# Adding transfers or vector sums for three outer sums, and one or two levels in the last down product of an expert

## The chip, the cores and the metric

The kernel runs on one core of a Trainium2 chip. The metric is the device time of one execution in microseconds, median of several runs. TensorE (PE) multiplies, VectorE (DVE), ScalarE (ACT) and GpSimd (POOL) do the elementwise work, SyncE (SP) issues plain transfers, and POOL issues the transfers that add to what lies at their destination. All data is float32.

## The reference, cut to what matters

```
kv  = einsum('bhsd,bhse->bhde', k, v)          # 8 x 8 heads, 576 rows, 64 columns
o   = einsum('bhsd,bhde->bhse', q, kv)
x   = (o / sqrt(mean(o*o, -1) + 1e-6) * g_norm)   # reshaped to 4608 x 512
p   = domain_probs / (domain_probs.sum(-1) + 1e-9)
out = 0
for e in range(4):
    h    = maximum(x @ w1[e], 0)               # 512 -> 1024: the "up" product
    out += p[:, e] * (h @ w2[e])               # 1024 -> 512: the "down" product
```

Almost all the time goes into the up and the down products of the four experts.

## The kernel before

The 4608 rows of x are cut into 9 chunks of 512. One step s = 9 e + c is expert e on chunk c, so there are 36 steps, 0 to 35. A step has an up product (`up`, line 851 on) and a down product, and the down product of step s runs beside the up product of step s + 1.

Both products use Strassen's scheme: 7 products of blocks in place of 8, with sums of blocks before and after. The up product uses it at two levels from step 1 on: 7 outer products m, in the order 1, 2, 6, 5, 3, 7, 4, each made of 7 inner products mm of two instructions (line 891). For one outer product, ScalarE copies four results out of the up banks of PSUM (`u1`, `u2`; L910) and one seed into another bank, and VectorE adds two others (`total`, L918) into one buffer, `made[m]`. The outer sums then join whole buffers of 128 x 1024:

- after m = 2: h1 = made1 + made2, then a Relu in place (L874)
- after m = 6: made1 and made6 are added, and later v, from that sum and made5
- after m = 4: h2 = made1 + made4, then a Relu
- others make h21, h4, h7, h5, h6, h3; these always are sums of VectorE, or of VectorE or GpSimd, whichever the planner finds free (`combine`, L360).

The down product has two forms. `down` (line 1100 on) is one level: 14 products of four instructions with 256 columns (L1118), whose results are scaled by p and merged straight out of PSUM (ACT L1065, DVE L1072) into the output blocks. `down_deep` (line 1140 on) is two levels: 98 instructions for the same, of 128 columns (L1193), with sums of h before them (L360), copies and sums out of PSUM (L1221, L1229) and sums of outer products after them (L1259). Both send output blocks off by transfers that add in DRAM (L1088), issued by GpSimd, in every expert but the first, step 35 left out.

In the kernel before, `down` serves the steps of the first expert and step 35, and `down_deep` serves steps 9 to 34. The three outer sums listed by name above (h1, made1 + made6, h2) are made by adding transfers from buffer to buffer (L867) in steps 9 to 33, and by `combine` in steps 1 to 8, 34 and 35.

At the change of an expert, steps 8, 17 and 26, the weights of the next one are loaded and their Strassen sums formed (`weights_1`, `weights_2` and its `inner`): sums of 128 x 1024 and of 128 x 256 on VectorE and GpSimd, in between the others.

The order on every engine is written out by a planner (`Plan.layout`), which simulates the engines with costs per operation and picks for each the ready operation that is due first; buffers are given out there too: 29 of the kind "big" (128 x 1024), to which 4 more come after the attention, 2 banks each of u1, u2, db and ab. The order of each engine is then fixed: an instruction that waits holds up all those behind it on its engine. For an adding transfer the planner counts

```
{"POOL": 1.0}     # and, as kb is set, 5.5 us more until its result is there
```

Of the kernel before, what the change touches and what calls it, by code (L numbers as in the profile page):

```python
# [10 lines left out]
ALU = mybir.AluOpType  # L11
# [219 lines left out]
def kernel(  # L231
# [36 lines left out]
    nc = tc.nc  # L268

    B, H, S, D = q.shape  # L270
    E, DM, F = moe_w1.shape
# [5 lines left out]
    NCH = B + 1  # L277
# [56 lines left out]
    plan = Plan()  # L334
# [4 lines left out]
    def dve(n):  # L339
        return {"DVE": 0.155 + 0.00104 * n}  # L340

    def act(n):
        return {"ACT": 0.155 + 0.00088 * n}
# [12 lines left out]
    def combine(key, cost, out_, a, b, op, reads, writes):  # L356

        plan.add(
            key, cost,
            lambda eng: adder(eng).tensor_tensor(out=out_(), in0=a(), in1=b(), op=op),  # L360
            reads=reads, writes=writes, port=True,
        )
# [488 lines left out]
    def up(s, e, views):  # L851
        made = {}
        h = {}

        def add(key, to, a, b, op=ALU.add, where=either):
            combine(
                key, where(2 * NT), lambda: to.ap[:], lambda: a.ap[:], lambda: b.ap[:], op,
                [a, b], [to],
            )

        by_dma = e > 0 and s < 34

        def accumulate(key, to, a):

            plan.add(
                key, {"POOL": 1.0},
                lambda eng: nc.gpsimd.dma_start(out=to.ap[:], in_=a.ap[:], accum_op=ALU.add),  # L867
                reads=[a, to], writes=[to], kb=512,
            )

        def relu(key, b):
            plan.add(
                key, act(2 * NT),
                lambda eng: nc.scalar.activation(out=b.ap[:], in_=b.ap[:], func=ACT.Relu),  # L874
                reads=[b], writes=[b],
            )

        for i, m in enumerate(OUTER):
            n = f"{s}_{m}"
            whole = made[m] = Buf("big", f"m{n}")  # L880
            bank = {
                1: Buf("u1", f"u1_{n}"), 2: Buf("u2", f"u2_{n}"), 5: Buf("u2", f"u3_{n}"),
            }
            snap = {}
            for j, mm in enumerate(ORDER):
                key = s + (i + j / 7) / 7
                ps = bank[{2: 2, 5: 5, 3: 5}.get(mm, 1)]

                def product(eng, m=m, mm=mm, ps=ps):
                    for u in range(2):  # L890
                        nc.tensor.matmul(  # L891
                            ps.ap[:, u * P:(u + 1) * P],
                            lhsT=w1f[e][m][mm][1]()[:, u * P:(u + 1) * P], rhs=views[m][mm][1](),
                            start=(mm in (1, 5) and u == 0), stop=True, skip_group_check=True,
                        )

                op = plan.add(
                    key, pe(2, P), product,
                    reads=w1f[e][m][mm][0] + [views[m][mm][0]] + ([ps] if mm == 2 else []),
                    **{"parts" if mm == 2 else "writes": [ps]},  # L900
                    after=last[-2:-1] if mm == 1 else seeds if mm == 5 else (),
                )
                op.marks, op.seed = (ps, HN), mm == 2
                if mm == 3:
                    last.append(op)

                def copy(to, where, ps=ps, key=key):
                    return plan.add(
                        key - 0.4, act(HN),
                        lambda eng: nc.scalar.activation(  # L910
                            out=where(), in_=ps.ap[:, 0:HN], func=ACT.Copy),
                        reads=[ps], parts=[to],
                    )

                def total(a, t, src, add_, whole=whole, key=key):
                    plan.add(
                        key - 0.4, dve(HN),
                        lambda eng: nc.vector.tensor_tensor(  # L918
                            out=block(whole, a, t), in0=src.ap[:, 0:HN], in1=add_.ap[:], op=ALU.add),
                        reads=[src, add_], parts=[whole],  # L920
                    )

                if mm == 1:
                    seeds = [copy(bank[2], lambda b=bank[2]: b.ap[:, 0:HN])]
                elif mm in (6, 7):
                    snap[mm] = Buf("snap", f"s{mm}_{n}")
                    copy(snap[mm], lambda b=snap[mm]: b.ap[:])
                if mm == 2:
                    copy(whole, lambda whole=whole: block(whole, 0, 0))
                elif mm == 7:  # L930
                    total(1, 1, bank[5], snap[7])
                elif mm == 4:
                    copy(whole, lambda whole=whole: block(whole, 1, 0))
                elif mm == 3:
                    total(0, 1, ps, snap[6])
            key = s + (i + 1) / 7

            def unit(f):
                h[f] = Buf("big", f"h{f}_{s}")
                return h[f]  # L940

            if m == 2 and by_dma:
                h[1] = made[2]
                accumulate(key, h[1], made[1])
                relu(key, h[1])
            elif m == 2:
                add(key, unit(1), made[1], made[2])
                relu(key, h[1])
            elif m == 6 and by_dma:
                accumulate(key, made[6], made[1])  # L950
                made[1] = made[6]
                made[6] = None
            elif m == 6:
                add(key, made[1], made[1], made[6])
            elif m == 5:
                made[6] = made[6] or Buf("big", f"v{s}")
                add(key, made[6], made[1], made[5])
            elif m == 3:
                add(key, unit(21), made[6], made[3])
                relu(key, h[21])  # L960
                add(key, unit(7), h[1], h[21], ALU.subtract)
            elif m == 7:
                add(key, made[1], made[1], made[7])
                add(key, unit(4), made[1], made[5], where=dve)
                relu(key, h[4])
                add(key, unit(5), h[21], h[4], where=dve)
                add(key, unit(6), h[5], h[1], ALU.subtract, dve)
            elif m == 4:
                if by_dma:
                    h[2] = made[4]  # L970
                    accumulate(key, h[2], made[1])
                else:
                    add(key, unit(2), made[1], made[4])
                relu(key, h[2])
                add(key, unit(3), h[2], h[6], ALU.subtract)
        hidden[s] = h
# [333 lines left out]
    for e in range(E):  # L1310
        for c in range(NCH):
            s = e * NCH + c
            if e == 0 and c + 1 < B:
                attention(c + 1, s - 0.1, 0.8, s + 0.5)
            if e + 1 < E and c == NCH - 1:
                weights_1(e + 1, s + 0.0, 0.12, s + 0.3)()
                inner[e + 1] = weights_2(e + 1, s + 0.6, 0.1, s + 1.3)
            if s + 1 < E * NCH:
                if e == 0 and c + 1 < NCH:
                    x_views[s + 1] = x_forms(c + 1, s + 0.7)  # L1320
                else:
                    x_views[s + 1] = x_again((c + 1) % NCH, s + (0.05 if e else 0.6), 0.13)
            if s:
                up(s, e, x_views.pop(s))
            if c == 0 and e:
                inner[e]()
            if e and s < E * NCH - 1:
                if not primed:
                    banks = [Buf("ab", f"prime{i}") for i in range(2)]

                    def prime(eng, banks=banks):
                        for b in banks:
                            nc.tensor.matmul(b.ap[:, 0:P], lhsT=ident[:], rhs=ident[:], start=True,
                                             stop=False, skip_group_check=True)
                            nc.tensor.matmul(b.ap[:, P:HN], lhsT=ident[:], rhs=ident[:], start=False,
                                             stop=True, skip_group_check=True)

                    primed.append(plan.add(s + 1.1, pe(4, P), prime, writes=banks))
                    primed[0].marks = banks[0], HN
                down_deep(s, e, c)  # L1340
            else:
                down(s, e, c)
# [7 lines left out]
    with tc.manual_schedule(engines={ENG.PE, ENG.DVE, ENG.Activation, ENG.Pool, ENG.SP}):  # L1350
# [4 lines left out]
        for op in order:  # L1355
# [6 lines left out]
            made = op.fn(op.eng)  # L1362
# [34 lines left out]
```

## Time and profile before

| | |
|---|---|
| median of 3 runs | 1745.47 us (1743.44 to 1745.48) |
| the profiled execution's own time | 1745.47 us |
| its span, first to last instruction | 1743.7 us |
| TensorE clock granted | 1.000 |
| DVE L360, 128 x 1024 sum of three big buffers | 216 of them, mean 1351 ns |
| POOL L360, the same | 42, mean 2354 ns |
| POOL L867, adding transfers | 75 issues (47 + 14 + 12 + 2 by kind of buffer), 512 KB each |
| issue to landing of these | 4.5 / 7.2 / 10.6 us (least, median, most) |
| waits of ACT L874 (Relu) for a transfer | 28.2 us in 18 waits |
| DMA queues | q1 191.21 MB, q0 (issued by GpSimd) 66.60 MB |

The page's first part gives the busy time of each engine, its share of the span and its instructions. The windows give the same for stretches of time, so that stages with different limits can be told apart. A line of a timeline has start, duration, engine, line, operation, and in square brackets how long the engine had been idle and what ended that. The durations of matmuls overlap, so the rate of TensorE is read from the spacing of their starts, and its idle time from the brackets.

### The profile page before, as it was taken

What the parts mean: (1) busy time and instruction counts of PE and PEld (TensorE: products, weight loads), DVE (VectorE), ACT (ScalarE), POOL (GpSimd) and SP (SyncE); (2) the same over time, 40 slices, a digit from 0 to 9 for tenths busy, and PEclk for the clock granted to TensorE, in tenths of its full rate; (3) what the DMA queues carried; (4) which work ended last, traced back from release to release, by engine and by line L of the source; (5) the groups of instructions that cost most, each with busy time, mean ns of one, the idle gap of its engine ahead of it and who ended that gap; (6) DMA issues with size and microseconds to landing.
All of it is one profiled execution on the core that took longest, in us unless ns stands there. A gap on an engine that the chain in (4) does not pass through costs nothing.

```text
span 1743.7 us, 39108 instructions
## 1 busy us (share of the span) xinstructions
PE 1721.8 (99%) x15502; PEld 1655.9 (95%) x15502; DVE 1151.2 (66%) x1961; ACT 947.2 (54%) x2340; POOL 667.8 (38%) x628
## 2 busy tenths in 40 slices
PE   9999999999999999999999999999999999999998
PEld 7699999999999999999999999999999999999998
DVE  4755655565685766666678876666678876666774
ACT  3445544454444656565555665556556665556662
POOL 2431332123343333343344543343444553343331
PEclk9999999999999999999999999999999999999999
DMA  9746543543345566666676665666685666656442
GB/s 235 227 152 191 165 134 109 185 140 140 127 146 133 134 141 147 133 150 137 166 215 146 141 144 133 145 146 146 153 234 134 146 145 146 146 135 147 119 110 49
DMA packets 159399, 260.31 MB, mean 149 GB/s; under 512 B 50800, under 2 KB 92016, under 8 KB 159216
## 3 DMA queue, kind: packets, MB, share of 16 engines
q1 hardware_dynamic: 133312, 191.21, 35.4%
q0 software_dynamic: 25904, 66.60, 22.2%
q8 instruction: 122, 2.00, 0.5%
q14 instruction: 61, 0.50, 0.1%
HBM read 145.30 MB, written 73.14 MB: 125 GB/s over the span
## 4 chain that ended last, share of the span: by engine, by line
PE 89%; DMA 7%; POOL 1%; ACT 1%; issue 1%; DVE 1%; POOLq 0%; ACTq 0%; DVEq 0%
PE u L891 40%; PE db L1193 17%; PE db L1118 13%; PE ab L1193 10%; DMA big<-big 5%; PE u L991 2%; PE ab L634 1%; DMA big<-small 1%; PE ab L1346 1%; PE ab L620 1%; PE ab L678 1%; PE ab L660 1%; POOL out_dram L1088 1%; PE u L1118 1%; DMA out_dram<-big 1%
## 5 line engine op out<-in xcount | busy, mean ns | idle before, releaser
L891 PE MATMUL u<-xf,big 128*128 128x128 f32 x3392 | 491.7, 276 | 8.4 <-ACT snap L910 8.4
L891 PEld LDWEIGHTS u<-xf,big 128*128 128x128 f32 x3392 | 435.3, 192 | 12.7 <-ACT snap L910 10.7
L360 DVE TENSOR_TENSOR big<-big,big 128x1024 f32<-128x1024 f32 (+1 forms) x391 | 380.0, 983 | 46.9 <-ACT big L874 26.6
L891 PE MATMUL u<-xf,w1y 128*128 128x128 f32 x2652 | 393.6, 277 | 3.0 <-DVE big L918 1.8
L891 PEld LDWEIGHTS u<-xf,w1y 128*128 128x128 f32 x2652 | 344.4, 192 | 7.2 <-DVE big L918 4.3
L918 DVE TENSOR_TENSOR big<-u,snap 128x256 f32<-128x256 f32 x430 | 181.1, 421 | 224.6 <-PE u L891 170.0
L910 ACT ACTIVATE snap<-u 128x256 f32<-128x256 f32 x490 | 187.3, 382 | 226.2 <-PE u L891 174.4
L1118 PE MATMUL db<-big,big 128*128 128x256 f32 x1040 | 246.0, 380 | 2.1 <-DVE big L560 2.1
L360 POOL TENSOR_TENSOR big<-big,big 128x256 f32<-128x256 f32 (+1 forms) x141 | 175.3, 1244 | 177.5 <-DVE big L360 80.8
L910 ACT ACTIVATE big<-u 128x256 f32<-128x256 f32 x430 | 164.6, 383 | 108.2 <-PE u L891 76.9
L1118 PEld LDWEIGHTS db<-big,big 128*128 128x128 f32 x1040 | 188.4, 191 | 22.3 <-DVE big L560 2.3
L1193 PE MATMUL db<-big,big 128*128 128x128 f32 x1088 | 154.2, 276 | 0.0
L874 ACT ACTIVATE big<-big 128x1024 f32<-128x1024 f32 x123 | 129.4, 1052 | 26.3 <-DMA big<-big 20.0
L1193 PEld LDWEIGHTS db<-big,big 128*128 128x128 f32 x1088 | 137.5, 192 | 0.3
L1221 ACT ACTIVATE snap<-db 128x256 f32<-128x256 f32 x208 | 74.0, 356 | 109.6 <-PE db L1193 108.6
L1193 PE MATMUL db<-kv,big 128*128 128x128 f32 x840 | 121.1, 276 | 0.8 <-ACT snap L1221 0.8
L360 DVE TENSOR_TENSOR big<-big 128x512 f32<-128x512 f32 (+1 forms) x111 | 85.6, 774 | 47.2 <-ACT big L874 45.8
L360 POOL TENSOR_TENSOR big<-big 128x512 f32<-128x512 f32 (+1 forms) x53 | 66.5, 1255 | 112.6 <-DVE big L360 76.4
L1193 PEld LDWEIGHTS db<-kv,big 128*128 128x128 f32 x840 | 107.2, 192 | 1.0 <-ACT snap L1221 1.0
L1229 DVE TENSOR_TENSOR big<-ab,snap 128x256 f32<-128x256 f32 x138 | 58.1, 421 | 73.2 <-ACT snap L1221 45.2
L910 ACT ACTIVATE u<-u 128x256 f32<-128x256 f32 x245 | 91.1, 372 | 26.4 <-PE u L891 6.8
L1088 POOL DMA_DIRECT2D out_dram<-big x102 | 94.3, 1091 | 13.2 <-ACT big L1065 9.3
(217 smaller groups left out, 2653.7 us busy)
## 6 DMA issues: line engine op xcount, KB each, us to landing
xf<-x SPq DMA_DIRECT2D x108, 512.0 KB, 3.8
big<-big POOLq DMA_DIRECT2D x47, 512.0 KB, 7.3
out_dram<-big POOLq DMA_DIRECT2D x86, 256.0 KB, 6.5
xf<-x_h SPq DMA_DIRECT2D x81, 256.0 KB, 3.5
xf<-x SPq DMA_DIRECT2D x81, 256.0 KB, 3.7
x<-xf SPq DMA_DIRECT2D x36, 512.0 KB, 6.8
big<-in_moe_w_dram SPq DMA_DIRECT2D x27, 512.0 KB, 5.1
small<-in_q_dram SPq DMA_DIRECT2D x72, 128.0 KB, 4.7
```

The lines of the kernel that those rows point to most:

```text
L360: lambda eng: adder(eng).tensor_tensor(out=out_(), in0=a(), in1=b(), op=op),
L620: nc.tensor.transpose(bank.ap[:, rs], qt.ap[:, rs], ident[:])
L874: lambda eng: nc.scalar.activation(out=b.ap[:], in_=b.ap[:], func=ACT.Relu),
L891: nc.tensor.matmul(ps.ap[:, u * P:(u + 1) * P], lhsT=w1f[e][m][mm][1]()[:, u * P:(u + 1) * P], rhs=views[m][mm][1](), start=(mm in (1, 5) ...
L910: lambda eng: nc.scalar.activation(out=where(), in_=ps.ap[:, 0:HN], func=ACT.Copy),
L918: lambda eng: nc.vector.tensor_tensor(out=block(whole, a, t), in0=src.ap[:, 0:HN], in1=add_.ap[:], op=ALU.add),
L991: nc.tensor.matmul(bank.ap[:], lhsT=two(w.ap[:])[:, kt, ut * P:(ut + 1) * P], rhs=two(xh[dh].ap[:])[:, kt, :], start=(dh == kt == 0), stop ...
L1088: nc.gpsimd.dma_start(out=dst, in_=cell(i)[parts, :], accum_op=ALU.add)
L1118: nc.tensor.matmul(ps.ap[:, 0:HN], lhsT=four(h[m])[:, kt // 2, t, kt % 2, :], rhs=w2f[e][m].ap[:, kt * HN:(kt + 1) * HN], start=(m in (1, ...
L1193: nc.tensor.matmul(ps.ap[:, o * P:(o + 1) * P], lhsT=b.ap[:, col:col + P], rhs=w2q[e][m][mm][1]()[:, kt, :], start=(mm in (1, 5) and o == ...
L1221: lambda eng: nc.scalar.activation(out=where(), in_=group_of(ps.ap), func=ACT.Copy),
L1229: lambda eng: nc.vector.tensor_tensor(out=cell(tq, dq), in0=group_of(src.ap), in1=group_of(add_.ap), op=ALU.add,),
```

## The change

Two things change. The three outer sums of steps 9 to 33 are no longer adding transfers but sums of `combine`, as in the other steps. And the down products of steps 17 and 26, the last chunks of the second and third expert, take the one-level form `down` in place of `down_deep`; step 35 had it already. The bank of the last step that the change's short name speaks of (`"u2" if s == E * NCH - 1`) is in both kernels.

```
-        by_dma = e > 0 and s < 34
-
-        def accumulate(key, to, a):
-
-            plan.add(
-                key, {"POOL": 1.0},
-                lambda eng: nc.gpsimd.dma_start(out=to.ap[:], in_=a.ap[:], accum_op=ALU.add),
-                reads=[a, to], writes=[to], kb=512,
-            )
-
...
-            if m == 2 and by_dma:
-                h[1] = made[2]
-                accumulate(key, h[1], made[1])
-                relu(key, h[1])
-            elif m == 2:
+            if m == 2:
                 add(key, unit(1), made[1], made[2])
                 relu(key, h[1])
-            elif m == 6 and by_dma:
-                accumulate(key, made[6], made[1])
-                made[1] = made[6]
-                made[6] = None
             elif m == 6:
                 add(key, made[1], made[1], made[6])
             elif m == 5:
-                made[6] = made[6] or Buf("big", f"v{s}")
                 add(key, made[6], made[1], made[5])
...
             elif m == 4:
-                if by_dma:
-                    h[2] = made[4]
-                    accumulate(key, h[2], made[1])
-                else:
-                    add(key, unit(2), made[1], made[4])
+                add(key, unit(2), made[1], made[4])
                 relu(key, h[2])
...
-            if e and s < E * NCH - 1:
+            if e and c < NCH - 1:
                 if not primed:
...
                 down_deep(s, e, c)
             else:
                 down(s, e, c)
```

## The prediction

> **What bounds the kernel now.** I read the engine table first, then the windows by stage, then TensorE's own idle times, and last ScalarE's queue just ahead of those. From the page and from the windows (columns of the latter: us, then busy time of PE, weight loads, DVE, ACT and POOL with instruction counts, clock, DMA share, GB/s):
>
> ```profile
> span 1743.7 us, 39108 instructions
> PE 1721.8 (99%) x15502; PEld 1655.9 (95%) x15502; DVE 1151.2 (66%) x1961; ACT 947.2 (54%) x2340; POOL 667.8 (38%) x628
> ```
>
> ```profile
> 700.00:750.00 50.00, 49.12 (x438) 48.74 (x437) 31.01 (x54) 28.54 (x73) 20.67 (x20) 1.00 0.64 143
> 850.00:900.00 50.00, 49.16 (x440) 48.97 (x439) 39.04 (x66) 27.63 (x74) 20.88 (x20) 1.00 0.78 206
> 900.00:950.00 50.00, 49.41 (x441) 49.09 (x440) 40.75 (x72) 28.88 (x75) 22.21 (x23) 1.00 0.62 147
> 1626.00:1714.00 88.00, 88.00 (x790) 88.00 (x789) 61.05 (x97) 53.40 (x134) 28.65 (x29) 1.00 0.43 103
> ```
>
> TensorE is the bound everywhere. A microsecond of product added or of TensorE idle taken away is a microsecond of the end; work on the others costs only where it makes TensorE wait. In the experts after the first (from about 510 us) it idles a little, up to 1.2 us in 50. The timeline of TensorE shows this as single gaps, 15 of them, 11.6 us together. What stands ahead of one, first on ScalarE, then on TensorE:
>
> ```profile
> 618.09 0.37 ACT L1221 ACTIVATE ab<-db 128x256 f32<-128x256 f32 x1 [0.45 <-PE db L1193]
> 620.66 1.06 ACT L874 ACTIVATE big<-big 128x1024 f32<-128x1024 f32 x1 [2.21 <-DMA big<-big]
> 621.62 0.36 ACT L910 ACTIVATE snap<-u 128x256 f32<-128x256 f32 x1
> ```
>
> ```profile
> 620.57 0.61 PE L1193 MATMUL ab<-big,small 128*128 128x128 f32 x4
> 622.04 0.71 PE L891 MATMUL u<-xf,big 128*128 128x128 f32 x4 [0.86 <-ACT snap L910]
> ```
>
> The Relu (L874) stands at the head of ScalarE's queue and waits 2.21 us for an adding transfer; the copies that free the up banks (L910) are behind it, and TensorE waits 0.86 us for one. The same picture stands ahead of 11 gaps (622, 711, 800, 846, 1067, 1113, 1157, 1426, 1470, 1516, 1560 us), with 0.86+0.81+0.41+0.61+0.81+0.35+0.93+0.99+0.80+1.18+0.63 = 8.4 us. The other four (884, 939, 1282, 1340) lie around the steps where the next expert's weights are formed, 3.3 us: three wait for a DVE sum (L918), one for a copy behind a wait for an output transfer. Ahead of that at 884, DVE waits 3.10 us for a weight load:
>
> ```profile
> 882.43 1.23 DVE L360 TENSOR_TENSOR big<-big,big 128x1024 f32<-128x1024 f32 x1 [3.10 <-DMA big<-in_moe_w_dram]
> ```
>
> **What the Trainium skill says.** "DMA: Bandwidth & Descriptors", section "SWDGE vs HWDGE vs iDMA", has adding transfers issued from GpSimd alone; the trace agrees, all 75 are on POOL's queue. "Perfetto Trace Analysis", section "Optimizing Scalar/DVE Operations", says GpSimd and DVE share an SBUF read port, so moving work between them might not help. The trace does not show the lock itself, but a 128x1024 sum is 1.35 us on DVE and 2.35 us on POOL, so neither is a free place.
>
> **The change, part by part.** I compared the written-out order of both programs. It changes three things.
>
> 1. *Two down products go from two levels to one* (steps 17 and 26; only step 35 did so in the later experts before). Instructions of L1193 fall from 2548 to 2352, those of L1118 rise from 560 to 672; the trace holds each twice (two passes). Durations there overlap, so I take the spacing: in the chain of waits 24 of L1193 fill the stretch from 1711.34 to 1714.02 us (0.1117 each), and 96 of L1118 that from 1718.37 to 1739.10 (0.2159). So 224 x 0.2159 - 392 x 0.1117 = 48.4 - 43.8 = **+4.6 us**, all on TensorE and all on the path. On DVE it removes 14 sums of L1259 (0.73), 16 of L1229 (0.29 to 0.42), 24 of 128x512 (0.85), 23 of 128x256 (about 0.45), and adds 12 merges of L1072 (0.48): 10 + 6 + 20 + 10 - 6 = 40 us less in two steps. 40 copies leave ScalarE (about 14 us), hidden before and after. That relief falls in the steps after 17 and 26, the second of the boundary windows.
>
> 2. *75 adding transfers become sums.* Per up product of steps 9 to 33 three sums change place, 73 net to DVE and 2 to POOL (10 of 128x512 more and 5 of 128x256 fewer go there too, as the planner shares out). DVE: 73 x 1.35 = +99 us, 4 us in each step of some 44 us. POOL loses 75 issues (46.4+14.4+10.5+2.4 = 74 us) and gains 2 x 2.35 + 10 x 1.3 - 5 x 0.75 = 14. The POOL queue then holds the output transfers and its own sums alone; nobody on TensorE's path waits for those issues other than the Relu. DMA loses 39 of the 66.6 MB of the software queue: no bound, but loads land no later. What the Relu waited for, 0.88 us of issue and a median of 7.2 us to landing, is now one DVE sum of 1.35 us. So the 11 gaps lose their cause: **-8.4 us**.
>    Is a sum on DVE then late? The trace holds the answer for two steps: steps 34 and 35 already add on DVE, beside two-level down products. The last adding transfer starts at 1626.5, and from 1626 to 1714 TensorE has no gap at all, with DVE 61 of 88 us busy (69%). Steady steps have about 31 of 50 now; with 4.6 more they come to 35, 71%. So I put new gaps in steady steps at zero; bounds 0 and one gap of 0.3 us in each of 20 steps, 6 us.
>
> 3. *Buffers.* h1 and h2 were made in place by the transfer and now take a buffer of their own (v, the other way round, is now made in place): up to two more of the 33 "big" ones for part of an up product. The trace shows no wait that is put down to buffers alone; the nearest is ScalarE's 2.88 us wait for an output transfer ahead of the gap at 1282 (0.84 us). Bounds: below zero (-0.8 us, if that gap goes with the lighter DMA) and 2 us at each of two expert boundaries. I take 0.
>
> What I can't read off is the boundary. In steps 17/18 and 26/27 DVE forms 128x1024 and 128x256 weight sums between the others, and is 39 to 41 of 50 us busy. Its order is fixed, so behind a weight sum that waits for its load stand the sums (L918) that free the up banks, and TensorE waits for those. In the window of step 17, 4.6 us more make 43.6 of 50; in step 18 the one-level product takes more away than the sums bring. The written-out order shows that DVE is late there: after the first product of step 17's down stage and the tail of step 16's, ten up products stand in a row in step 18 (and 27) before the second one, and soon four down products follow each other. As long as up products are at hand TensorE does not idle. Bounds: 0, if they cover it all, and 5 us at each boundary, if the 3.10 us wait for a weight load and a queue of two sums (2.7 us) reach TensorE less the 0.84 it already costs. I take 2 us each: **+4 us**.
>
> Sum against the profiled execution's own time, 1745.47 us (its span of 1743.7 and 1.8 around it), which is also the median of the three runs: 4.6 - 8.4 + 4 = +0.2, so 1745.7, say **1746 us**. With no new gap -3.8, with both upper bounds of boundary and steady steps 4.6 - 8.4 + 10 + 6 = +12.2.
>
> **The rivals.** A measurement of this kernel can tell about 0.2%, 3.5 us, from no change: 1742.0 to 1749.0.
>
> *As worked out: within that.* What the transfers cost ScalarE's queue pays for the lower saving of two down products. For it: both terms rest on counted instructions or listed gaps. 40%; own range 1742 to 1749.
>
> *DVE sets the pace at the expert boundaries: slower.* Place: DVE's queue in steps 17/18 and 26/27. A sum that the queue used not to hold stands ahead of L918; with 6 us of slack in 50, part of it already spent on waits for weights, DVE stays behind, banks come free late, and TensorE idles for as long. For it: DVE at 78 to 82% there, and three gaps that already wait for L918. Against it: the same windows lost only 0.8 us each, and step 18 is relieved by about 20 us. At 5 us per boundary: 1745.5 + 4.6 - 8.4 + 10 = 1751.7; with gaps in steady steps 1757.7. It decides from 7.3 us of new gaps on. 35%.
>
> *No new gaps: faster.* If boundaries behave like steps 34 and 35, only 4.6 and -8.4 are left: 1741.7; if the gap at 1282 or that at 884 goes too with the lighter DMA load, 1740.9. For it: the clean 88 us. Against: neither step forms weights. 25%.
>
> *That sums don't go where the diff seems to send them* (to POOL, at 2.35 us) is excluded by the order: 2 of 75. And the bank of the last step named in the change's title is in both kernels and moves nothing.
>
> **Numbers.** The likeliest case gives 1746. The range runs from 1740 (no new gaps, one or two old ones gone as well, 1 us of spread) to 1758 (the slower rival with gaps in steady steps): about 2 in 10 lie outside, more of it above.
>
> **What would show each step right or wrong.** Right: L1118 at 1344 matmul records and L1193 at 4704, TensorE busy about 4.6 us longer for the same gaps; no "ACT big L874 <- DMA" rows among the waits (28 us now) and none of the 11 gaps; DVE near 1210 us, POOL near 608. Wrong in the boundary term: gaps on TensorE between the start of step 17 and the end of step 18 that sum to well over 2 us, with "DVE big L918" or a down product as what they wait for. Wrong in the second part: a gap in most steady steps with DVE as releaser. Wrong in the first: spacing of L1118 in those steps other than 1.73 us per eight.

## The result, and the profile after

The changed kernel takes 1730.51 us (median of 4 runs, 1729.95 to 1730.74) against 1744.45 us (1742.59 to 1745.48) of the kernel before: ratio 0.9921, 95% interval 0.9904 to 0.9938. It is faster by 14 us, where 1746 and no change were forecast, and lies below the range. In a later session it took 1730.31 us.

The engine table of the page after, and the start of its chain of waits:

```profile
span 1728.2 us, 38444 instructions
PE 1718.7 (99%) x15334; PEld 1651.4 (96%) x15334; DVE 1224.7 (71%) x1969; ACT 939.3 (54%) x2300; POOL 614.8 (36%) x560
```

```profile
PE 99%; POOL 1%; DVE 0%; ACT 0%; issue 0%; POOLq 0%
```

TensorE's busy time fell by 3.1 us although 4.6 us of products were added. This is the first sign that "busy" hides something. (The lines of the changed kernel have other numbers: L881 is L891 of the kernel before, L900 is L910, L908 is L918, L864 is L874, L1170 is L1193 and L1095 is L1118.) Windows of the kernel after (columns as before: us, busy time and count of PE, weight loads, DVE, ACT, POOL, then clock, DMA share, GB/s):

```profile
700.00:750.00 50.00, 50.00 (x451) 50.00 (x450) 36.89 (x61) 30.22 (x76) 18.82 (x18) 1.00 0.48 116
850.00:900.00 50.00, 50.00 (x450) 50.00 (x450) 43.15 (x62) 27.69 (x75) 22.08 (x20) 1.00 0.66 190
900.00:950.00 50.00, 50.00 (x361) 47.52 (x360) 40.79 (x66) 28.26 (x67) 26.46 (x27) 1.00 0.46 107
```

Compare the count of matmuls in the first line with that of the same window before: 451 now, 438 then, both of 128 columns. 13 matmuls at 0.1117 us are 1.45 us, but the busy time before was only 0.88 us below 50. The count tells what was lost, the busy time does not. (In the third line many have 256 columns, so its count is lower at full rate.) TensorE's timeline has no bracket from 78 us to the last product.

### Reading the loss from the spacing of starts

Three lines of TensorE's timeline of the kernel before show where the difference sits:

```profile
620.57 0.61 PE L1193 MATMUL ab<-big,small 128*128 128x128 f32 x4
622.04 0.71 PE L891 MATMUL u<-xf,big 128*128 128x128 f32 x4 [0.86 <-ACT snap L910]
622.83 0.94 PE L891 MATMUL u<-xf,w1y 128*128 128x128 f32 x6
```

A group of four takes 0.447 us at full rate. From 620.57 to 622.04 are 1.47 us, a loss of 1.02, where the bracket says 0.86: a matmul is shown as lasting 276 ns, but the next one starts after 112 ns, so its shown end reaches 164 ns into the gap. And the four after the gap take 0.79 us, another 0.34, with no bracket at all. Of these, 0.10 is lost between the first and the second matmul, and 0.24 in a second short wait ahead of 622.83, for a sum of VectorE (L918); it shows as only 75 ns of idle time, and the timeline prints no bracket below 150 ns. So idle time, as it was read before the change, is not the time lost. From here on "lost" is the sum over all matmuls from 520 us on of the distance to the next start less 0.1117 us (128 columns) or 0.2161 us (256 columns). It is 20.3 us in the kernel before, where the brackets add up to 11.6, and 0.03 us after. With the 4.6 us of added products the span should shrink by 15.7; it shrank by 15.5.

### The profile page after: what moved, and what is told of

It is laid out like the page before. It is cut to its first block, busy times and chain, and to the rows that moved or that the text cites. A ratio compares the mean times of both kernels' runs of the same rounds, so it can differ in the third digit from the quotient of the medians.

```text
span 1728.2 us, 38444 instructions
## 1 busy us (share of the span) xinstructions
PE 1718.7 (99%) x15334; PEld 1651.4 (96%) x15334; DVE 1224.7 (71%) x1969; ACT 939.3 (54%) x2300; POOL 614.8 (36%) x560
## 4 chain that ended last, share of the span: by engine, by line
PE 99%; POOL 1%; DVE 0%; ACT 0%; issue 0%; POOLq 0%
PE u L881 45%; PE db L1170 19%; PE db L1095 14%; PE ab L1170 12%; PE ab L1095 2%; PE u L968 2%; PE ab L634 1%; PE ab L1323 1%; PE ab L620 1%; PE ab L678 1%; PE ab L660 1%; PE u L1095 1%; POOL rt L551 0%; PE db L660 0%; PE ab L722 0%; PE ab L704 0%
## 5 line engine op out<-in xcount | busy, mean ns | idle before, releaser
L360 DVE TENSOR_TENSOR big<-big,big 128x1024 f32<-128x1024 f32 (+1 forms) x450 | 442.5, 997 | 36.0 <-ACT big L864 23.8
L881 PE MATMUL u<-xf,big 128*128 128x128 f32 x3104 | 453.0, 275 | 0.0
L881 PEld LDWEIGHTS u<-xf,big 128*128 128x128 f32 x3104 | 401.3, 192 | 2.2
L881 PE MATMUL u<-xf,w1y 128*128 128x128 f32 x2652 | 389.6, 275 | 0.0
L908 DVE TENSOR_TENSOR big<-u,snap 128x256 f32<-128x256 f32 x430 | 181.5, 422 | 235.1 <-PE u L881 175.7
L881 PEld LDWEIGHTS u<-xf,w1y 128*128 128x128 f32 x2652 | 343.4, 192 | 2.2
L900 ACT ACTIVATE snap<-u 128x256 f32<-128x256 f32 x490 | 188.1, 384 | 251.3 <-PE u L881 213.9
L1095 PE MATMUL db<-big,big 128*128 128x256 f32 x1120 | 264.1, 380 | 2.1 <-DVE big L560 2.1
L1095 PEld LDWEIGHTS db<-big,big 128*128 128x128 f32 x1120 | 202.9, 190 | 24.6 <-DVE big L560 2.3
L900 ACT ACTIVATE big<-u 128x256 f32<-128x256 f32 x430 | 165.0, 384 | 110.4 <-PE u L881 74.3
L360 POOL TENSOR_TENSOR big<-big,big 128x256 f32<-128x256 f32 (+1 forms) x138 | 170.2, 1241 | 131.6 <-DVE big L360 44.1
L1170 PE MATMUL db<-big,big 128*128 128x128 f32 x1056 | 146.7, 275 | 0.0
L864 ACT ACTIVATE big<-big 128x1024 f32<-128x1024 f32 x128 | 134.4, 1050 | 2.6 <-POOL big L360 1.3
L1170 PEld LDWEIGHTS db<-big,big 128*128 128x128 f32 x1056 | 132.1, 192 | 0.1
L1236 POOL TENSOR_TENSOR big<-big 128x512 f32<-128x512 f32 x26 | 32.9, 1266 | 269.2 <-DVE big L360 263.9
L1198 ACT ACTIVATE snap<-db 128x256 f32<-128x256 f32 x192 | 68.5, 357 | 99.8 <-PE db L1170 94.9
L1170 PE MATMUL db<-kv,big 128*128 128x128 f32 x804 | 114.6, 275 | 0.0
L900 ACT ACTIVATE u<-u 128x256 f32<-128x256 f32 x245 | 90.9, 371 | 27.9 <-PE u L881 8.0
L1170 PEld LDWEIGHTS db<-kv,big 128*128 128x128 f32 x804 | 102.1, 192 | 0.1
```

Source lines behind the costliest of these rows:

```text
L881: nc.tensor.matmul(ps.ap[:, u * P:(u + 1) * P], lhsT=w1f[e][m][mm][1]()[:, u * P:(u + 1) * P], rhs=views[m][mm][1](), start=(mm in (1, 5) ...
L900: lambda eng: nc.scalar.activation(out=where(), in_=ps.ap[:, 0:HN], func=ACT.Copy),
L908: lambda eng: nc.vector.tensor_tensor(out=block(whole, a, t), in0=src.ap[:, 0:HN], in1=add_.ap[:], op=ALU.add),
L1095: nc.tensor.matmul(ps.ap[:, 0:HN], lhsT=four(h[m])[:, kt // 2, t, kt % 2, :], rhs=w2f[e][m].ap[:, kt * HN:(kt + 1) * HN], start=(m in (1, ...
L1170: nc.tensor.matmul(ps.ap[:, o * P:(o + 1) * P], lhsT=b.ap[:, col:col + P], rhs=w2q[e][m][mm][1]()[:, kt, :], start=(mm in (1, 5) and o == ...
L1198: lambda eng: nc.scalar.activation(out=where(), in_=group_of(ps.ap), func=ACT.Copy),
```

## The experiments

The theory: a Relu (L874) that waits for an adding transfer at the head of ScalarE's queue holds up the copies behind it, TensorE waits for these, and the planner put it there because it counts on the result too early: 1.0 us for the issue and 5.5 us more, 6.5 in all, while the trace has a median of 7.2 from the start of the issue to landing (45 of the 75 take more than 6.5). The rivals: the relief of VectorE at the expert boundaries is the gain; or the transfers cost by their number and load on DMA, SBUF and GpSimd, wherever the Relu stands.

| kernel | transfers | planner's count after the issue | steps 17, 26 | added products | lost | span | median |
|---|---|---|---|---|---|---|---|
| before | 75 | 5.5 us | two levels | 0 | 20.3 | 1743.7 | 1744.5 to 1745.4 |
| after | 0 | - | one level | 4.6 | 0.0 | 1728.2 | 1730.5 |
| sums only | 0 | - | two levels | 0 | 6.9 | 1730.8 | 1733.0 |
| down only | 75 | 5.5 | one level | 4.6 | 17.4 | 1746.3 | 1752.8 |
| told late | 75 | 8.5 | two levels | 0 | 8.6 | 1732.7 | 1735.5 |
| h1 and h2 | 50 | 5.5 | two levels | 0 | 27.7 | 1751.5 | 1753.0 |
| made1 + made6 | 25 | 5.5 | two levels | 0 | 5.5 | 1729.4 | 1731.1 |
| told early | 75 | 2.5 | two levels | 0 | 70.6 | 1794.5 | 1798.2 |
| told late, one level | 75 | 8.5 | one level | 4.6 | 8.6 | 1737.2 | 1741.2 |
| boundary steps only | 12 | 8.5 | two levels | 0 | 1.1 | 1724.7 | 1726.5 |
| all but 17 and 26 | 69 | 8.5 | two levels | 0 | 2.0 | 1726.0 | 1727.0 |

All in us; "lost" and the span are those of the profiled execution. In every row 1743.7 - 20.3 + added products + lost gives the span within 1 us (told late: 1732.0 against 1732.7; told early: 1794.0 against 1794.5). So products and lost time explain the spans.

**The sums alone.**

```
-            if e and c < NCH - 1:
+            if e and s < E * NCH - 1:      # on the changed kernel
```

> The sums alone: the three outer sums by combine, two-level down products kept in steps 17 and 26. Theory 1 (Relus that wait for adding transfers hold up ScalarE's copies and so TensorE; spacing of matmul starts puts the loss of before at 20.3 us, 13.9 of it at the 11 Relu gaps): the loss leaves with the transfers, and the 4.6 us of one-level products don't come: 1744.5 - 20.3 = 1724, up to 1729 if the gaps at the expert boundaries (4.3 us) stay. Rival (the gain comes from the one-level products, which relieve VectorE at the boundaries): above 1736, with new gaps in steps 17/18 and 26/27, as VectorE has 20 us more work in each of them than the changed kernel.

1733.01 us, ratio 0.9932 (0.9916 to 0.9949). Between the two expectations and in neither: the sums alone bring 12 us of the gain. But here 6.9 us are lost after the boundaries, most of it around 954, 1044, 1339, 1352 and 1442 us, and the largest row among TensorE's waits of that part names VectorE. That row (us in total, times, longest us) and a window:

```profile
PE u L881 <- DVE big L908: 2.6, 3, 1.0
```

```profile
950.00:1000.00 50.00, 49.11 (x436) 48.54 (x435) 41.50 (x77) 31.61 (x79) 24.92 (x21) 1.00 0.38 96
```

So in the changed kernel the one-level products earn their 4.6 us: without them 6.9 us are lost. How they do it is not shown. VectorE is as busy with them as without: 1224.7 us in the changed kernel and 1225.2 here, as the planner gave it other sums in the place of those that went. GpSimd has 22.2 us less (614.8 against 637.0) and ScalarE 12.3 less, and the order is another one.

**The down products alone.**

```
-            if e and s < E * NCH - 1:
+            if e and c < NCH - 1:          # on the kernel before
```

> The down products alone: one level in steps 17 and 26, adding transfers kept. Theory 1: the Relu gaps stay, the products add 4.6 us, at most the boundary gaps (4.3 us) go: 1745 to 1749. Rival (boundary relief is the gain): 1730 to 1738.

1752.82 us, ratio 1.0042 (1.0024 to 1.0060): slower, above what the theory gave. The profiled run, 1748.1, was the fastest of five, so what the others lost beyond its 17.4 us is not seen. The Relus wait as before, here 20 and 3 times:

```profile
ACT big L874 <- DMA big<-big: 30.7, 20, 3.4
ACT big L874 <- DMA big<-small: 4.9, 3, 2.1
```

By itself this half of the change is no gain: the median is 8 us longer, with 4.6 us of added products. The first rival falls as the main cause; that the one-level products help once the sums are on VectorE, the run before this one shows.

**The planner told of a later landing.**

```
 if op.kb:
-    op.end += 5.5
+    op.end += 8.5 if op.kb == 512 else 5.5
```

> The kernel before with all 75 adding transfers and all two-level products, but the planner counts 8.5 us in place of 5.5 from issue to result for them (the trace has a median of 7.2 and at most 10.6 us), so that it places the Relus later in ScalarE's order. Theory 1, in the form that the wrong latency in the planned order is the cause: the gaps go, 1744.5 - 14 = 1730, within 4. Rival (the transfers cost by their load on DMA, SBUF and GpSimd, wherever the Relu stands): 1740 to 1746.

1735.51 us, ratio 0.9947 (0.9932 to 0.9962), with every transfer and every two-level product still there. That is 1.5 us above the range of the theory and below that of the rival. In steady steps nothing is lost any more, and no Relu waits for a transfer. ScalarE's timeline at the place where TensorE lost time at 711, first in the kernel before, then here:

```profile
709.83 1.06 ACT L874 ACTIVATE big<-big 128x1024 f32<-128x1024 f32 x1 [2.15 <-DMA big<-small]
710.79 0.36 ACT L910 ACTIVATE snap<-u 128x256 f32<-128x256 f32 x1
```

```profile
708.13 0.38 ACT L910 ACTIVATE snap<-u 128x256 f32<-128x256 f32 x1
709.09 0.38 ACT L1221 ACTIVATE big<-ab 128x256 f32<-128x256 f32 x1 [0.57 <-PE ab L1193]
709.53 0.37 ACT L910 ACTIVATE u<-u 128x256 f32<-128x256 f32 x1
709.92 0.38 ACT L910 ACTIVATE big<-u 128x256 f32<-128x256 f32 x1
710.20 1.05 ACT L874 ACTIVATE big<-big 128x1024 f32<-128x1024 f32 x1
```

The copies now stand ahead of the Relu, and it starts without a wait. And TensorE, beside just as many transfers, runs at full count:

```profile
700.00:750.00 50.00, 50.00 (x450) 50.00 (x449) 32.63 (x57) 29.79 (x75) 16.13 (x17) 1.00 0.68 151
```

So in steady steps of this run the transfers cost TensorE nothing by their load. The 8.6 us that stay lie at the boundaries (882 and 954 to 976, 1273 to 1276, 1357 and 1373 us).

**Only the sums that a Relu reads by transfer.**

```
-            elif m == 6 and by_dma:
+            elif m == 6 and False:
```

> 50 of the 75 adding transfers kept, those whose result a Relu reads (h1 and h2); the third, made1 + made6, by combine; two-level products kept. Theory 1: nearly all of the loss stays, 1738 to 1745. Rival (loss in proportion to the number of transfers): a third of 20.3 us goes, 1737.7.

1753.00 us, ratio 1.0039 (1.0024 to 1.0054): a third of the transfers fewer, and more is lost, 27.7 us. The theory expected the loss to stay, not to grow; in proportion to the number it would have shrunk. Why it grew is open: the planner makes another order, in which Relus wait for transfers 23 times in place of 18.

```profile
ACT big L874 <- DMA big<-big: 36.2, 20, 3.0
PE u L891 <- ACT snap L910: 12.0, 13, 1.7
```

**Only the sum that no Relu reads by transfer.**

```
-            if m == 2 and by_dma:
+            if m == 2 and False:
...
-                if by_dma:
+                if False:
                     h[2] = made[4]
```

> 25 adding transfers kept, those of made1 + made6, which no Relu reads; h1 and h2 by combine; two-level products kept; planner's latency as before (5.5 us). Theory 1 (Relus at the head of ScalarE's queue): no Relu waits for a transfer, 1727 to 1735, with the boundary gaps of the sums-only kernel (6.9 us). Rival (any adding transfer that lands later than planned delays the chain of sums, through VectorE): gaps with VectorE as the releaser in many steps, above 1738.

1731.10 us, ratio 0.9920 (0.9905 to 0.9935): as the theory has it, with 5.5 us lost, nearly all at the boundaries and just behind them. Among its waits there is none of L874 for a transfer.

**The planner told of an earlier landing.**

```
-    op.end += 5.5
+    op.end += 2.5 if op.kb == 512 else 5.5
```

> The kernel before, but the planner counts 2.5 us in place of 5.5 for an adding transfer, while the chip takes 7.2. Theory 1: the Relus stand further ahead in ScalarE's order, each waits some 3 us longer, most of the 50 in steps 9 to 33 now reach TensorE: loss well over 20.3 us, 1770 to 1850. Rival (the transfers' load or their number is the cost, not the place of the Relu): the same as before, within 5 us of 1745.

1798.18 us, ratio 1.0299 (1.0273 to 1.0325). The same operations, only in an order that trusts the transfers more, lose 70.6 us in place of 20.3:

```profile
ACT big L874 <- DMA big<-big: 76.7, 36, 4.7
PE u L891 <- ACT snap L910: 27.0, 21, 2.4
PE db L1193 <- ACT snap L1221: 13.8, 4, 4.2
```

2.5, 5.5 and 8.5 us in the planner give 70.6, 20.3 and 8.6 us lost. (Of the 70.6, 11.9 us lie in stretches in which TensorE's clock was at half, behind some of its longer waits; see the last section.) The edit changes the whole written-out order and the times at which buffers come free, not the place of the Relus alone. But the Relus' waits come and go with the loss (28.2 us before, none at 8.5, 94 at 2.5), and where transfers feed no Relu, steady steps lose next to nothing. The main cause is shown by this: not the transfer, but the place in a fixed order of what waits for it.

**Told late, with one-level products.**

The two edits of "told late" and "down only" together.

> All 75 adding transfers, planner told 8.5 us, and one-level down products in steps 17 and 26: the changed kernel with transfers in place of sums. Theory 1: steady steps lose nothing (as in the run told 8.5 us with two levels), the boundary losses of that run (8.5 us) mostly go with the relief, the products add 4.6: 1730 to 1735. Rival (transfers cost by their load): clearly above, 1738 or more.

1741.22 us, ratio 0.9974 (0.9964 to 0.9984): a miss for the theory as written, and in the range of the rival. But steady steps lose nothing, beside as many transfers as before; the loss is elsewhere: the boundary keeps 8.6 us. Timelines of VectorE and TensorE there show another wait:

```profile
885.09 1.23 DVE L360 TENSOR_TENSOR big<-big,big 128x1024 f32<-128x1024 f32 x1 [6.29 <-DMA big<-in_moe_w_dram]
```

```profile
886.71 1.22 PE L891 MATMUL u<-xf,w1y 128*128 128x128 f32 x4 [4.47 <-DVE big L918]
```

The weight sum at the head of VectorE's queue waits 6.29 us for its load, the sum (L918) that frees an up bank is behind it, and TensorE waits 4.47 us. It is the pattern of the Relu on another engine. SP issued that load at 872.51 us; it is the fourth of these loads, and it landed 12.49 us later. In the changed kernel the fourth was issued at 869.64 and landed after 8.84, and no sum of VectorE waits for one.

**Transfers in all steps but 17 and 26.**

```
-        by_dma = e > 0 and s < 34
+        by_dma = 0 < e and s < 34 and s % NCH < NCH - 1     # told 8.5 us
```

> Adding transfers in steps 9 to 33 but for 17 and 26, where the weights of the next expert are loaded; planner told 8.5 us, two-level products kept. Theory A (the losses that stay at the boundary in the runs told 8.5 us come from transfers that share the DMA engines with the weight loads in those steps): they go, 1726 to 1730. Theory B (they come from the written-out order, which sets when a weight load is issued and who waits behind the sum that reads it): they stay in some form, 1732 to 1738.

1727.04 us, ratio 0.9891 (0.9875 to 0.9908): theory A in its size. Six transfers fewer take away 6.6 of the 8.6 us that told late still lost. But the next run has transfers in just these steps and loses no more, so their presence beside weight loads is not enough. Taking them out also changes the order and the buffers. The fourth weight load is issued at 872.51 us, as in told late with one level, but lands after 8.06 us in place of 12.49, and VectorE waits 0.59 us for it in place of 6.29. So at this boundary it was a slower landing and not a later issue that made VectorE wait longer in the one run than in the other; why it was slower, the transfers beside it or something else, stays open. And this run keeps 69 of the 75 transfers and is still 3.3 us faster than the changed kernel, which has none (1730.31 us on the same chip): the transfers as such are not what the kernel before lost its time by.

**A version that beats both.**

```
-        by_dma = e > 0 and s < 34
+        by_dma = s in (17, 18, 26, 27)      # told 8.5 us, two levels kept
```

> Towards a version that beats both: two-level products in steps 9 to 34, sums by combine, and adding transfers only in the steps around a change of expert, 17, 18, 26 and 27 (12 transfers), planner told 8.5 us. Theory 1: VectorE is relieved of 4 us in each of these steps, so of the 6.9 us that the sums-only kernel lost there about half goes: 1727 to 1730. Rival (what lands late at the boundary are weight loads and output transfers, not sums): 1732 to 1736.

1726.48 us, ratio 0.9893 (0.9878 to 0.9907). This is a little below the 1727 to 1730 of the theory, as most of the 6.9 us are gone and not half. Two-level products stay in steps 17 and 26, so the 4.6 us are saved as well. Whether it is the relief of VectorE is not shown: twelve sums less would be some 16 us, but VectorE is busy for 1223.1 us against 1225.2 with sums only, and the order is another one. The same windows as above:

```profile
850.00:900.00 50.00, 50.00 (x448) 49.84 (x448) 42.76 (x64) 27.15 (x73) 23.44 (x23) 1.00 0.73 199
900.00:950.00 50.00, 50.00 (x450) 50.00 (x449) 40.63 (x74) 29.91 (x79) 24.38 (x25) 1.00 0.58 140
```

Then both once more, on one chip:

> The changed kernel, unaltered, beside the next one on the same chip, so that the two can be told apart: 1729 to 1732.

> The kernel with sums, two-level products in steps 9 to 34 and adding transfers in steps 17, 18, 26 and 27 alone, planner told 8.5 us, unaltered: if its 4.0 us over the changed kernel are its own and not the chip's, 1725 to 1728 and the interval below that of the changed kernel; else the two are within 1 us.

The changed kernel: 1730.31 us (1729.74 to 1730.51). This version: 1726.69 us (1726.36 to 1726.99), 3.6 us less, with no overlap. It loses 0.8 to 1.1 us, so with these products little is left to gain from the order in this part.

## Why the prediction was wrong

**Held.** TensorE was read rightly as the bound. Matmul records came to 1344 of the one-level product and to 4704 of the two-level one, as counted; the +4.6 us of part 1 is confirmed by the sum of span, products and lost time. The cause named for the 11 gaps is the right one, and replacing the transfers removed all of them: no Relu waits for a transfer any more. The load of the first boundary window (43.15 us of 50, 43.6 forecast) is near. Steady steps run without a gap, as read off steps 34 and 35.

**Near by luck.** DVE (1224.7 us, 1210 forecast) and POOL (614.8, 608). The forecast added 99 us to DVE for the sums and took 40 off for the one-level products, and took 60 off POOL for the transfers. Going by the run with sums only, the sums added 74 to DVE and took 31 off POOL, and the one-level products took 0.5 off DVE and 22 off POOL. The planner shares out again whatever comes free, so the parts are not as forecast, and their errors cancel in part.

**Failed, the size of a gap.** The step is "a microsecond of TensorE idle taken away", taken from the brackets: 8.4 us for the 11 gaps. By spacing of starts these 11 lost 13.9 us. That is 5.5 of the 15.7 us between the forecast's +0.2 and the -15.5 measured between the two profiled executions. Another 2.1 us were lost in eight places for which the list of gaps had nothing; four of them, with 1.3 us, stand behind a Relu's wait for a transfer too. The prediction had the better reading at hand in the lines it showed, as counts of matmuls in a window: 438 in 50 us, against 790 in the 88 us without a gap, which is 449 in 50.

**Failed, the other four gaps.** The sum has only the -8.4 and leaves them in place. They lost 4.3 us and went too; the faster rival had allowed for one of two of them. Of the cases, "no new gaps" was the one that happened, but with 4.6 - 20.3 = -15.7 in place of its -3.8.

**Failed, the boundary term.** +4 us for VectorE coming late in steps 17/18 and 26/27. Measured: 0, although VectorE is busy 81 to 86% in these windows, against 77 to 82% in those where the kernel before had gaps. So the step from a busy VectorE to a late bank did not hold. The relief by the one-level products was taken for an argument against and then not used in the sum, and the run with sums but two-level products does lose 6.9 us, at these places and in the two steps behind them. So the worry was not empty; the change carries its own remedy, though not as the 40 us less of VectorE work that were counted. The ten up products in a row seen in the written-out order were no sign of a stall: TensorE had them at hand. The four terms, 5.5 + 2.1 + 4.3 + 4.0 = 15.9, make up the 15.7 by which the forecast missed, but for the rounding.

In the same way the slower rival failed: its price assumed that 3.10 us of waiting for weights and two sums reach TensorE. Such a case exists, but in other orders (6.29 us of wait and 4.47 us on TensorE, in told late with one level).

## What to carry to other kernels

Where an engine's order is fixed ahead by estimated times, an operation whose latency is underestimated costs little itself; what it costs is the queue behind the instruction that waits for it, so check each estimate against the landing times of a trace, and lean to the late side. Price a stall of a pipelined engine by the spacing of starts, or by the count of instructions in a window against a full one, not by its idle brackets: here 20.3 us against 11.6. And when a change moves work onto a loaded engine and takes other work off it in the same stretch, test the halves apart: one half (sums) gave 12 us, the other alone cost 8, and together they gave 14.

## What the runs showed of the hardware

- The first matmul after a wait is followed late by the second: at 622.04 us in the kernel before, the second started 0.21 us after it in place of 0.11. All 15 gaps of that kernel show it.
- Behind some waits TensorE's clock drops to half for a while. In told late with one level it was granted 0.50 for 3.41 us from 886.52 us on, where the bracket of 4.47 us ends, and matmuls of 128 columns started 0.213 us apart in place of 0.112. This cost 1.6 of the 8.6 us lost there. Told early has 27.3 us of such stretches, with 11.9 us lost, and told late one of 3.41 us at 1275.79. In these three runs all four waits with brackets of 3.3 to 4.5 us were followed by one, and of eight with 2.0 to 2.5 us four were (2.03, 2.05, 2.21, 2.41) and four not (2.01, 2.30, 2.35, 2.41). The kernel before and the changed kernel have none between 520 us and the last product.
- Runs in which Relus wait for transfers spread more: 1748.1 to 1756.5 us for the down products alone, 1792.2 to 1800.2 told early. It is not the number of transfers: with 69 of them and no such wait the runs lie between 1726.46 and 1727.78, and the changed kernel, with none, between 1729.95 and 1730.74.
